# Retention attention, a gated layer and a two-layer MLP on one Trainium2 core: the rest scores of a pair moved behind the far parts, weight steps re-dealt, gelu's table loaded first

## The chip, the cores and the metric

The kernel runs on one core of one Trainium2 chip. The metric is device time in microseconds, the median of three runs; lower is better. The core has TensorE (PE, with its weight loads as PEld), VectorE (DVE), ScalarE (ACT), GpSimd (POOL), and SyncE (SP), whose queue issues every transfer of this kernel.

## What is computed

Three layers in a row, all in fp32 (products of the two later layers are made of three products of high and low halves):

```python
# attention: B, H, S, D = 4, 8, 576, 64
scores = q @ k.T / sqrt(64);  ret = scores * gamma_h ** (i - j)  (0 where i < j);  x = ret @ v
# gated layer: x is [4, 576, 512], d_ff = 1024
h = gelu_tanh(x @ w_in);  u, v = split(h);  v = layernorm(v) * g_ln
x = x + (u * (w_sg @ v + b_sg)) @ w_out
# two-layer MLP
x = x + relu((layernorm(x) * g_ln2) @ w_ch1) @ w_ch2
```

The weights w_in, w_out and w_ch reach the device as pairs of 32-bit words (float64) and are turned into fp32 there.

## The kernel before, in words

**Attention.** The 32 heads are taken as 16 units of two heads; `for k in range(NPAIR)` runs over eight pairs of units, a = 2k and b = 2k + 1. The 576 positions are four chunks of 128 and a rest of 64. For each unit `scores` makes the products of q and k within the chunks (L254; one PSUM bank for each head), `masks` multiplies them on DVE into p and frees these banks (L260), `states` makes k times v of each chunk (L294), `scans` runs the decayed sum over chunks on DVE (L304), `near` multiplies p with v (L316), and `far` adds the part that comes from earlier chunks (L325). The rest of 64 has its own steps, for both units of a pair in one bank: `scores_rest` (L273), `mask_rest` (L280) and `attend_rest` (L340). `finish(k)` is `far` and `put` (copy to SBUF by ACT, L347) of both units, then `attend_rest` and `put_rest` (L353). It runs one pair late: `finish(k - 1)` stands in the iteration of pair k. `scale_q` multiplies q by a row of decays on POOL, in two instructions: the four chunks (L241) and the rest (L243); this needs the scores to have been made, and `far` and `attend_rest` need it.

**PSUM.** There are eight banks. One is lent for good to the float64 conversion (`f64_at`), seven go round in a first-in, first-out list: `bank()` takes the oldest free one, `free` gives one back. While a pair runs, its four score banks, the two outputs of the pair ahead and the rest bank of the pair ahead are seven.

**Loads.** kk and qv tiles hold a unit's k and q with v; there are four kk and six qv buffers. The tiles of pair k + 2 are asked for in pair k, qv after `finish(k - 1)`, kk after `near`. All transfers are issued by SP in program order, so one that waits for its buffer holds up those behind it.

**Background.** `bg` is a generator that converts the weights in pieces of 512 columns, four steps a piece: a step that asks for the raw words two pieces ahead (L145) and makes the first DVE operation (L154); one that splits the piece before into high (ACT, L362) and low (POOL, L363) and makes the second DVE operation (L158); one with ACT's Square (L160) and DVE's third (L161); and one with DVE's last (L163). The very first step only asks for two raw pieces. Eight pieces are w_in, four w_out, and then w_ch follows to the end of the gated layer. `PAIR` says, for each pair, how many steps are made at its first place (ahead of `finish`) and at its last (behind `near`); `PACE` says the same for the gated layer.

**After attention.** `v_tile` makes the v half of the gated layer for batch 0: five products (tiles 0, 4, 1, 2, 3), each followed on ACT by gelu (L685), a squared sum (L670), the normalisation (L682) and the cast into a high half (L710); POOL makes the low half (L711). The steps of one tile's normalisation come some `tick`s after its gelu, between the next ones. `u_chunk` makes the u half (eight products of 12 matmuls), and `sg_chunk` multiplies w_sg with the normalised v: each half is 4 x 3 + 2 = 14 matmuls, the last of them with tile 4's low half (L788). `load_sg` and `split_sg` load and split the five row tiles of w_sg.

The lines of every instruction follow the order of the code; each engine works through its own in that order.

Of the kernel before, what the change touches and what calls it, by code (L numbers as in the profile page):

```python
# [14 lines left out]
ACTF = mybir.ActivationFunctionType  # L15
ALU = mybir.AluOpType
# [5 lines left out]
NP = H // 2  # L22
F1 = 1024
F2 = 2048
C = 128
NC = S // C
R = S - NC * C
# [17 lines left out]
    "1112",  # L45
)
LATE = 5
PAIR = "00 01 00 23 23 23 24 35".split()

HIDDEN = {  # L50
    5: (5, 0, True, True), 0: (0, 1, True, False), 1: (1, 1, False, True), 2: (2, 2, True, False),
# [23 lines left out]
O_LATE = H  # L75
# [26 lines left out]
def kernel(  # L102
# [28 lines left out]
    def col(t, o, n=1):  # L131
        return t[:, o:o + n]
# [104 lines left out]
    def scale_q(n):  # L237
        q = units[n]["qT"]
        row = col(tab, O_LATE + n % NP * C, C)
        x = q[:, 0:NC * C].rearrange("p (c i) -> p c i", c=NC)  # L240
        pool.tensor_tensor(out=x, in0=x, in1=row.unsqueeze(1).to_broadcast([128, NC, C]), op=ALU.mult)  # L241
        x = q[:, NC * C:]
        pool.tensor_tensor(out=x, in0=x, in1=row[:, 0:R], op=ALU.mult)  # L243

    half = [slice(h * D, (h + 1) * D) for h in range(2)]

    def scores(n):
        unit(n)
        u = units[n]
        u["sc"] = [bank() for h in range(2)]  # L250
        for c in range(NC):
            j = slice(c * C, (c + 1) * C)
            for h in range(2):
                pe.matmul(u["sc"][h][:, j], u["kT"][half[h], j], u["qT"][half[h], j], start=True, stop=True)  # L254

    def masks(n):
        u = units[n]
        p = u["p"] = pa.tile([128, 2, NC, C], F32, tag="p", name="p")
        for h in range(2):
            dve.tensor_tensor(  # L260
                out=p[:, h], in0=u["sc"][h].rearrange("p (c i) -> p c i", c=NC),
                in1=mask[:, 2 * (n % NP) + h].unsqueeze(1).to_broadcast([128, NC, C]), op=ALU.mult,
            )
            free(u["sc"][h])
# [3 lines left out]
    def scores_rest(k):  # L268
        t = rests[k] = bank()
        for x in range(2):  # L270
            u = units[2 * k + x]
            for r in half:
                pe.matmul(  # L273
                    t[r, x * R:(x + 1) * R], u["kT"][r, NC * C:], u["qT"][r, NC * C:], start=True, stop=True,
                    skip_group_check=True,
                )

    def mask_rest(k):
        pr = units[2 * k]["pr"] = pa.tile([128, 2 * R], F32, tag="pr", name="pr")
        dve.tensor_tensor(  # L280
            out=pr, in0=rests[k][:, 0:2 * R], in1=col(tab, O_MASKR + 2 * k % NP * R, 2 * R), op=ALU.mult
        )
# [47 lines left out]
    def attend_rest(k):  # L330
        for part in range(2):
            for x in range(2):
                u = units[2 * k + x]
                for r in half:
                    o = rests[k][r, (2 + x) * R:(3 + x) * R]
                    if part == 0:
                        w, z = u["v"][r, NC * C:], units[2 * k]["pr"][r, x * R:(x + 1) * R]
                    else:
                        w, z = u["y"][r, NC - 1], u["qT"][r, NC * C:]
                    pe.matmul(o, w, z, start=part == x == 0, stop=part == 1, skip_group_check=True)  # L340
# [9 lines left out]
    def put_rest(k):  # L350
        b, hp = divmod(2 * k, NP)
        t = rests.pop(k)
        act.copy(xb[b][:, hp:hp + 2, NC * C:], t[:, 2 * R:4 * R].rearrange("p (x i) -> p x i", x=2))  # L353
        free(t)
        for x in range(2):
            del units[2 * k + x]
# [26 lines left out]
    def load_sg(part):  # L383
        if part == 0:
            w = S + NC * C + D
            t = [ld.tile([128, w], F32, tag="qv", bufs=6, name="raw_sg") for _ in range(2)]
            sg.extend(x[:, i * S:(i + 1) * S] for x in t for i in range(2))
        else:
            sg.append(ld.tile([128, S + NC * C], F32, tag="kk", bufs=4, name="raw_sg")[:, 0:S])
        for k in range(part * NC, NC + part):  # L390
            nc.sync.dma_start(out=sg[k], in_=w_sg[k])

    def split_sg(k):
        if k == 0:
            for t in [slot("w_sg") for _ in range(3)]:
                sg_rows.extend(t[:, a * S:(a + 1) * S] for a in range(3))
        if k < NC:
            wsl.append((sg_rows[2 * k], sg_rows[2 * k + 1]))
            split(sg_rows[2 * k], sg_rows[2 * k + 1], sg[k])
        else:  # L400

            t = sg_rows[8]
            wsl.append(t)
            act.copy(t, sg[k])
            pool.tensor_tensor(out=t[R:, :], in0=sg[k][R:, :], in1=f(t[R:, :]), op=ALU.subtract)
# [79 lines left out]
    def background(n):  # L485
        for _ in range(n):
            next(bg, None)
# [22 lines left out]
    for n in range(1, 4):  # L510
        load(load_kk(n), load_qv(n))

    act.copy(zero[:, 0:1], zero[:, 0:1])

    warm = bank()
    for _ in range(WARM):
# [40 lines left out]
            out=to, in0=to, in1=first[:, O_GR:O_GR + NP].unsqueeze(2).to_broadcast([128, NP, R]), op=ALU.mult  # L557
        )

    def finish(k):  # L560
        for n in (2 * k, 2 * k + 1):
            far(n)
            put(n)
        attend_rest(k)
        put_rest(k)

    for k in range(NPAIR):
        a, b = 2 * k, 2 * k + 1
        if k == 0:
            form_rows()  # L570
            form_masks(0)
        scores(a)
        if k == 0:
            scale_k(a)
        masks(a)
        if k == 0:
            form_decay()
            form_late()
            free(each[0])
            states(a)  # L580
            near(a)
            form_masks(1)
            free(each[1])
        else:
            scale_k(a)
        if k == 1:
            finish(k - 1)
        scores(b)
        masks(b)
        scale_k(b)  # L590
        scores_rest(k)
        if k:
            mask_rest(k)
        scale_q(a)
        scale_q(b)
        background(int(PAIR[k][0]))
        if k > 1:
            finish(k - 1)
        if 0 < k < NPAIR - 2:
            load(load_qv(a + 4), load_qv(b + 4))  # L600
        if k == NPAIR - 2:
            load_sg(0)
        if k == NPAIR - 1:
            split_sg(0)
            split_sg(1)
        if k:
            states(a)
        states(b)
        scans(k)
        if k == 0:  # L610
            form_rest()
            mask_rest(k)
        if k:
            near(a)
        near(b)
        if k == 0:
            load(load_kk(4), load_qv(4), load_kk(5), load_qv(5))
        else:
            load(load_kk(a + 4), load_kk(b + 4))
        if k == NPAIR - 2:  # L620
            load_sg(1)
        background(int(PAIR[k][1]))
        if k == NPAIR - 3:
            nc.sync.dma_start(out=par, in_=params)
        if 1 < k < 6:
            split_x(0, [k - 2])
        if k == 6:
            split_rest(0)
    finish(NPAIR - 1)
    background(4)  # L630
    for k in range(2, NC + 1):
        split_sg(k)
    background(4)
    es_a.close()

# [927 lines left out]
```

## Time and profile before

| what | value |
|---|---|
| median of three runs | 661.36 us (660.23 to 662.06) |
| the profiled execution, device time | 659.58 us |
| its span | 657.7 us |
| PE busy in the span | 646.3 us (98%) |
| DVE / ACT / POOL busy | 456.3 / 316.8 / 321.7 us |
| granted TensorE clock | 1.0 in every slice (the 2.4 GHz level) |

The span is what the profile shows of the program; 1.88 us of the profiled execution lie around it. PE is busy nearly all the time, so what counts are the few places where it is not. The timeline of an engine gives start and length of each merged group of instructions, and in brackets the idle time before it with what ended it.

### The profile page before, as it was taken

To read this page: it belongs to the slowest core of one execution; us is meant where nothing else is said; L and a number is where in the kernel's file an instruction comes from. 1 tells how busy PE (TensorE), PEld (TensorE's weight loads), DVE (VectorE), ACT (ScalarE), POOL (GpSimd) and SP (SyncE) were. 2 spreads that over 40 slices of the span, in tenths; PEclk is the share of its full clock that TensorE was granted. 3 is DMA by queue.
4 is the path that set the end of the run, shared out by engine and by line. 5 is a ranking of instruction groups with operands and counts; after the bars stand their busy time and mean duration, and the time that the engine had idled before them with its cause. 6 is when DMAs were issued, how large, how long until landed. Compare 5 with 4: busy or idle time off the path is not lost.

```text
span 657.7 us, 12552 instructions
## 1 busy us (share of the span) xinstructions
PE 646.3 (98%) x4422; PEld 590.2 (90%) x4422; DVE 456.3 (69%) x907; ACT 316.8 (48%) x657; POOL 321.7 (49%) x314
## 2 busy tenths in 40 slices
PE   8999998999999999999999999999999999999997
PEld 5998898899889889899888899988998889999996
DVE  5599879789889885868888633555533445458894
ACT  4465795375276457434453533233535313335443
POOL 2567767235226527955655693365558842410000
PEclk9999999999999999999999999999999999999999
DMA  8999537677697695489896768699999799999734
GB/s 312 409 386 327 189 98 231 225 251 235 214 307 228 190 236 141 170 296 389 311 301 251 265 204 272 242 371 379 340 323 346 242 303 322 360 370 412 281 129 160
DMA packets 99264, 181.22 MB, mean 276 GB/s; under 512 B 9857, under 2 KB 46849, under 8 KB 97410
## 3 DMA queue, kind: packets, MB, share of 16 engines
q1 hardware_dynamic: 99202, 180.42, 80.6%
q8 instruction: 35, 0.57, 0.3%
q14 instruction: 27, 0.22, 0.1%
HBM read 122.97 MB, written 56.62 MB: 273 GB/s over the span
## 4 chain that ended last, share of the span: by engine, by line
PE 84%; DVE 6%; ACT 5%; issue 3%; POOL 2%; DMA 1%; DVEq 0%; SPq 0%; POOLq 0%; ACTq 0%
PE b L137 22%; PE b L136 22%; PE b L135 22%; PE b L854 6%; PE b L1331 3%; PE b L1332 2%; PE b L325 1%; PE b L254 1%; DVE b L154 1%; DVE c L163 1%; PE b L294 1%; ACT raw L160 1%; PE b L316 1%; POOL vnl L711 1%; PE b L788 1%
## 5 line engine op out<-in xcount | busy, mean ns | idle before, releaser
L135 PE MATMUL b<-fe,w 128*128 128x384 f32 x336 | 113.2, 337 | 0.0
L137 PE MATMUL b<-fe,w 128*128 128x384 f32 x336 | 113.0, 336 | 0.0
L136 PE MATMUL b<-fe,w 128*128 128x384 f32 x336 | 112.7, 335 | 0.0
L137 PE MATMUL b<-w,h 128*128 128x512 f32 (+1 forms) x270 | 98.1, 363 | 0.0
L136 PE MATMUL b<-w,h 128*128 128x512 f32 (+1 forms) x270 | 97.9, 363 | 0.0
L135 PE MATMUL b<-w,h 128*128 128x512 f32 (+1 forms) x270 | 96.8, 358 | 0.0
L935 POOL TENSOR_TENSOR w<-raw_w,w 128x512 fp32r<-128x512 f32 x30 | 39.9, 1332 | 57.9 <-ACT w L934 50.8
L135 PEld LDWEIGHTS b<-fe,w 128*128 128x128 f32 x336 | 63.1, 188 | 4.0 <-DVE t L1188 0.8
L136 PEld LDWEIGHTS b<-fe,w 128*128 128x128 f32 x336 | 63.1, 188 | 2.6
L137 PEld LDWEIGHTS b<-fe,w 128*128 128x128 f32 x336 | 63.0, 188 | 0.0
L137 PEld LDWEIGHTS b<-w,h 128*128 128x128 f32 x270 | 50.9, 189 | 7.7
L160 ACT ACTIVATE raw<-raw 128x512 f32<-128x512 f32 x44 | 29.9, 680 | 57.7 <-DVE b L158 47.6
L136 PEld LDWEIGHTS b<-w,h 128*128 128x128 f32 x270 | 50.9, 189 | 6.1
L135 PEld LDWEIGHTS b<-w,h 128*128 128x128 f32 x270 | 51.0, 189 | 6.0 <-issue 0.2
L1165 ACT ACTIVATE h<-b 128x384 fp32r<-128x384 f32 x32 | 15.7, 491 | 79.5 <-DVE b L1194 53.1
L655 POOL TENSOR_TENSOR st<-st,par 128x1 f32<-128x1 f32 x36 | 22.1, 616 | 50.4 <-DVE st L654 50.3
L951 POOL TENSOR_TENSOR raw_turn<-raw_turn 128x256 f32<-128x256 f32 x32 | 23.6, 739 | 31.1 <-DMA raw_turn<-w_dram 20.8
L137 PE MATMUL b<-w_sg,vnl 128*128 128x288 f32 x128 | 37.8, 295 | 0.5 <-POOL vnl L711 0.5
L1166 DVE SCALAR_TENSOR_TENSOR h<-b,h 128x384 fp32r<-128x384 f32 x32 | 17.8, 556 | 29.4 <-ACT h L1165 29.4
L135 PE MATMUL b<-w_sg,vnh 128*128 128x288 f32 x128 | 37.8, 295 | 0.0
L137 PE MATMUL b<-xt_hi,w_in 128*128 128x288 f32 x128 | 37.7, 295 | 0.0
L136 PE MATMUL b<-w_sg,vnh 128*128 128x288 f32 x128 | 37.7, 295 | 0.0
(200 smaller groups left out, 1716.4 us busy)
## 6 DMA issues: line engine op xcount, KB each, us to landing
w<-ws_dram SPq DMA_DIRECT2D x96, 256.0 KB, 5.1
raw<-in_w_ch_dram SPq DMA_DIRECT2D x32, 512.0 KB, 5.0
ws_dram<-w SPq DMA_DIRECT2D x16, 896.0 KB, 7.3
w<-wb_dram SPq DMA_DIRECT2D x14, 1024.0 KB, 6.2
qv<-in_attn_dram SPq DMA_DIRECT2D x15, 576.0 KB, 6.4
w_dram<-c SPq DMA_DIRECT2D x32, 256.0 KB, 3.1
wb_dram<-fe SPq DMA_DIRECT2D x32, 256.0 KB, 5.4
kk<-in_attn_dram SPq DMA_DIRECT2D x15, 544.0 KB, 7.3
```

What stands on the lines that cost most here:

```text
L135: pe.matmul(ps, lh, rh, start=first, stop=False, skip_group_check=True)
L136: pe.matmul(ps, lh, rl, start=False, stop=False, skip_group_check=True)
L137: pe.matmul(ps, ll, rh, start=False, stop=last, skip_group_check=True)
L160: act.activation(out=f(w1), in_=f(w1), func=ACTF.Square)
L655: pool.tensor_tensor(out=st[:, 4:5], in0=st[:, 3:4], in1=col(par, O_MH), op=ALU.pow)
L854: pe.matmul(ps, g, wo[k][:, w], start=done[0] == 1, stop=done[0] == 3 * KE, skip_group_check=True)
L935: pool.tensor_tensor(out=t[:, 1], in0=raw, in1=f(t[:, 0]), op=ALU.subtract)
L951: pool.tensor_tensor(out=to, in0=y, in1=z, op=ALU.subtract)
L1165: act.activation(out=t[:, 0], in_=v, func=ACTF.Relu)
L1166: dve.scalar_tensor_tensor(out=t[:, 1], in0=v, scalar=0.0, in1=f(t[:, 0]), op0=ALU.max, op1=ALU.subtract)
L1331: pe.matmul(ps, e[:, 0, x], t, start=begin, stop=False, skip_group_check=True)
L1332: pe.matmul(ps[:, 0:256], e[:, 1, x], t[:, 0:256], start=False, stop=end, skip_group_check=True)
```

## The change

`scores_rest(k)` moves into `finish(k - 1)`, between `attend_rest` and `put_rest`, for pairs 2 to 7 (pairs 0 and 1 keep it behind `scores(b)`). Since `scale_q` may not overwrite the rest of q before that, the rest's multiplication becomes `scale_rest`, and it and `mask_rest(k)` now follow `finish(k - 1)`. `PAIR` is re-dealt: the first step, which asks for the first two raw pieces of w_in, is made at the end of pair 0 and not of pair 1, every pair from the second on makes half a piece at its end and the other half in the next pair, and four steps that stood between the attention and the gated layer are dropped there, so they are made later. Four of the five splits of w_sg now stand in the last pair (before: two). The first ACT instruction, a copy of one zero, becomes a gelu of it.

```diff
-PAIR = "00 01 00 23 23 23 24 35".split()
+PAIR = "01 02 22 22 22 22 22 34".split()
...
-        x = q[:, NC * C:]
-        pool.tensor_tensor(out=x, in0=x, in1=row[:, 0:R], op=ALU.mult)
+
+    def scale_rest(n):
+        x = units[n]["qT"][:, NC * C:]
+        pool.tensor_tensor(out=x, in0=x, in1=col(tab, O_LATE + n % NP * C, R), op=ALU.mult)
...
-    act.copy(zero[:, 0:1], zero[:, 0:1])
+    act.activation(out=zero[:, 0:1], in_=zero[:, 0:1], func=ACTF.Gelu_apprx_tanh)
...
-    def finish(k):
+    def finish(k, more=True):
         for n in (2 * k, 2 * k + 1):
             far(n)
             put(n)
         attend_rest(k)
+        if more:
+            scores_rest(k + 1)
         put_rest(k)
...
         if k == 1:
-            finish(k - 1)
+            finish(k - 1, False)
         scores(b)
+        if k == 1:
+            scores_rest(k)
         masks(b)
         scale_k(b)
-        scores_rest(k)
-        if k:
-            mask_rest(k)
+        if k == 0:
+            scores_rest(k)
         scale_q(a)
         scale_q(b)
         background(int(PAIR[k][0]))
         if k > 1:
             finish(k - 1)
+        if k:
+            mask_rest(k)
+        scale_rest(a)
+        scale_rest(b)
...
         if k == NPAIR - 1:
-            split_sg(0)
-            split_sg(1)
+            for x in range(2):
+                split_sg(x)
...
+        if k == NPAIR - 1:
+            for x in range(2, NC):
+                split_sg(x)
         background(int(PAIR[k][1]))
...
-    finish(NPAIR - 1)
-    background(4)
-    for k in range(2, NC + 1):
-        split_sg(k)
+    finish(NPAIR - 1, False)
+    split_sg(NC)
     background(4)
```

How the instructions stand, at three places. First PE in the last pair, from its last score product on; b_80, b_82 and so on are PSUM banks. Before:

```order
L254 MATMUL b_77<-qv,kk 128x128
L273 MATMUL b_82<-qv,kk 64x64 x4
L325 MATMUL b_81<-qv,y 64x128 x6
L325 MATMUL b_79<-qv,y 64x128 x6
L340 MATMUL b_80<-pr,qv 64x64 x4
L340 MATMUL b_80<-qv,y 64x64 x4
L294 MATMUL b_76<-qv,kk 64x64 x16
```

and now:

```order
L256 MATMUL b_77<-qv,kk 128x128
L327 MATMUL b_81<-qv,y 64x128 x6
L327 MATMUL b_79<-qv,y 64x128 x6
L342 MATMUL b_80<-pr,qv 64x64 x4
L342 MATMUL b_80<-qv,y 64x64 x4
L275 MATMUL b_82<-qv,kk 64x64 x4
L296 MATMUL b_76<-qv,kk 64x64 x16
```

The rest scores into b_82 moved from ahead of the far parts to behind `attend_rest`; pairs 2 to 6 read alike. DVE beside it, from the scans of pair 6 to those of pair 7 (b_75 is the conversion's bank, p the masked scores). Before:

```order
L304 SCALAR_TENSOR_TENSOR y<-formed,b_77 128x256 x2
L158 SCALAR_TENSOR_TENSOR b_75<-raw,b_75 128x512
L161 SCALAR_TENSOR_TENSOR b_75<-raw,b_75 128x512
L163 SCALAR_TENSOR_TENSOR c<-raw,b_75 128x512
L154 TENSOR_SCALAR b_75<-raw 128x512
L260 TENSOR_TENSOR p<-b_82,formed 128x512
L260 TENSOR_TENSOR p<-b_76,formed 128x512
L260 TENSOR_TENSOR p<-b_78,formed 128x512
L260 TENSOR_TENSOR p<-b_77,formed 128x512
L280 TENSOR_TENSOR pr<-b_82,tab 128x128
```

and now:

```order
L306 SCALAR_TENSOR_TENSOR y<-formed,b_77 128x256 x2
L154 TENSOR_SCALAR b_75<-raw 128x512
L158 SCALAR_TENSOR_TENSOR b_75<-raw,b_75 128x512
L262 TENSOR_TENSOR p<-b_82,formed 128x512
L262 TENSOR_TENSOR p<-b_76,formed 128x512
L262 TENSOR_TENSOR p<-b_78,formed 128x512
L262 TENSOR_TENSOR p<-b_77,formed 128x512
L161 SCALAR_TENSOR_TENSOR b_75<-raw,b_75 128x512
L163 SCALAR_TENSOR_TENSOR c<-raw,b_75 128x512
L154 TENSOR_SCALAR b_75<-raw 128x512
L282 TENSOR_TENSOR pr<-b_82,tab 128x128
```

Two conversion operations instead of four now stand between the scans and the next masks, and two stand between the masks and the rest's mask (a third, L154, in the last pair only).

Second, ACT from the end of the last pair's copies to the first gelu of the gated layer (b_78, b_77 and b_82 hold the last pair's outputs). Before:

```order
L347 COPY xb<-b_78 128x512
L347 COPY xb<-b_77 128x512
L353 COPY xb<-b_82 128x2x64
L362 CAST w_in<-c 128x512
L160 ACTIVATE raw<-raw 128x512
L362 CAST w_in<-c 128x512
L362 CAST w_sg<-raw_sg 128x576 x2
L404 CAST w_sg<-raw_sg 128x576
L160 ACTIVATE raw<-raw 128x512
L646 ACTIVATE par<-par 128x8
L685 ACT_TABLE_LOAD
L685 ACTIVATE t,st<-b_81 128x512
```

and now:

```order
L349 COPY xb<-b_78 128x512
L349 COPY xb<-b_77 128x512
L355 COPY xb<-b_82 128x2x64
L406 CAST w_sg<-raw_sg 128x576
L364 CAST w_in<-c 128x512
L160 ACTIVATE raw<-raw 128x512
L364 CAST w_in<-c 128x512
L656 ACTIVATE par<-par 128x8
L695 ACTIVATE t,st<-b_81 128x512
```

Two w_sg casts, one Square and the table load have left this stretch.

Third, SP in the first pairs, from the kk tile of unit 4 on. Before:

```order
L210 DMA kk<-in_attn_dram 128x1088
L217 DMA qv<-in_attn_dram 128x1152
L210 DMA kk<-in_attn_dram 128x1088
L217 DMA qv<-in_attn_dram 128x1152 x3
L210 DMA kk<-in_attn_dram 128x1088 x2
L145 DMA raw<-in_w_in_dram 128x1024 x2
L217 DMA qv<-in_attn_dram 128x1152 x2
L210 DMA kk<-in_attn_dram 128x1088 x2
L145 DMA raw<-in_w_in_dram 128x1024
```

and now:

```order
L210 DMA kk<-in_attn_dram 128x1088
L217 DMA qv<-in_attn_dram 128x1152
L210 DMA kk<-in_attn_dram 128x1088
L217 DMA qv<-in_attn_dram 128x1152
L145 DMA raw<-in_w_in_dram 128x1024 x2
L217 DMA qv<-in_attn_dram 128x1152 x2
L210 DMA kk<-in_attn_dram 128x1088 x2
L145 DMA raw<-in_w_in_dram 128x1024
L217 DMA qv<-in_attn_dram 128x1152 x2
```

The first two raw pieces now go ahead of the tiles of units 6 and 7, and from then on one raw piece more than before is ahead of each pair's tiles.

## Rows read from the trace of the kernel before

**Rows 1.** Busy us by engine in three stretches, then clock, DMA share, GB/s

```profile
core 0: us, PE busy (x) PEld busy (x) DVE busy (x) ACT busy (x) POOL busy (x), PEclk, DMA share, GB/s
...
22.52:71.44 48.92, 46.92 (x907) 44.38 (x905) 41.19 (x70) 28.02 (x59) 33.59 (x36) 1.00 0.94 351
...
97.86:102.62 4.76, 2.64 (x16) 1.98 (x15) 4.03 (x7) 3.74 (x9) 4.11 (x4) 1.00 0.79 215
102.62:600.00 497.38, 497.25 (x2736) 456.38 (x2736) 334.75 (x662) 225.36 (x460) 259.25 (x246) 1.00 0.84 280
```

**Rows 2.** PE's waits over the span: total us, times, longest us

```profile
PE b L273 <- DVE p L260: 2.0, 4, 1.1
PE b L788 <- POOL vnl L711: 1.5, 1, 1.5
```

**Rows 3.** PE timeline of pair 2: start, length, line, form; no wait inside

```profile
22.52 2.06 PE L254 MATMUL b<-qv,kk 64*128 64x128 f32 x32
...
24.80 1.65 PE L325 MATMUL b<-qv,y 64*64 64x128 f32 x24
...
27.08 1.15 PE L294 MATMUL b<-qv,kk 128*64 128x64 f32 x32
...
29.91 2.06 PE L254 MATMUL b<-qv,kk 64*128 64x128 f32 x32
```

**Rows 4.** PE timeline: starts of pairs 4, 5 and 7, and the last far parts

```profile
37.30 2.06 PE L254 MATMUL b<-qv,kk 64*128 64x128 f32 x32
...
45.09 2.06 PE L254 MATMUL b<-qv,kk 64*128 64x128 f32 x32
...
60.55 2.06 PE L254 MATMUL b<-qv,kk 64*128 64x128 f32 x32
...
69.10 1.71 PE L325 MATMUL b<-qv,y 64*64 64x128 f32 x24
```

**Rows 5.** DVE timeline: scans, masks of pair 3, a conversion step, masks of pair 7

```profile
28.27 1.26 DVE L304 TENSOR_TENSOR_SCAN y<-formed,b 128x256 f32<-128x256 f32 x2 [1.83 <-PE b L294]
...
31.16 2.48 DVE L260 TENSOR_TENSOR p<-b,formed 128x512 f32<-128x512 f32 x4 [1.62 <-issue]
...
62.37 0.69 DVE L154 TENSOR_SCALAR b<-raw 128x512 uint32<-128x512 uint32 x1
62.97 2.47 DVE L260 TENSOR_TENSOR p<-b,formed 128x512 f32<-128x512 f32 x4
```

**Rows 6.** PE timeline: first product of the u half, first of w_sg

```profile
85.14 0.29 PE L135 MATMUL b<-xt_hi,w_in 128*128 128x288 f32 x1
...
97.86 0.29 PE L135 MATMUL b<-w_sg,vnh 128*128 128x288 f32 x1
```

**Rows 7.** ACT timeline around the end of attention, first and fifth gelu

```profile
68.02 1.29 ACT L362 CAST w_sg<-raw_sg 128x576 fp32r<-128x576 f32 x2
...
75.47 1.25 ACT L362 CAST w_sg<-raw_sg 128x576 fp32r<-128x576 f32 x2
...
77.97 1.28 ACT L685 ACT_TABLE_LOAD   x1
79.26 0.60 ACT L685 ACTIVATE t<-b 128x512 f32<-128x512 f32 x1
...
88.04 0.59 ACT L685 ACTIVATE t<-b 128x512 f32<-128x512 f32 x1
```

**Rows 8.** POOL timeline: the last low half of v in batch 0

```profile
101.08 1.26 POOL L711 TENSOR_TENSOR vnl<-t,vnh 128x512 fp32r<-128x512 f32 x1
```

**Rows 9.** DMA issues at 14.08 (unit 5) and 20.45 (unit 6): KB, us to landing

```profile
qv<-in_attn_dram SPq DMA_DIRECT2D x1, 576.0 KB, 8.3
...
kk<-in_attn_dram SPq DMA_DIRECT2D x1, 544.0 KB, 6.4
```

**Rows 10.** As rows 1, two stretches of attention: DMA at its fullest and thinnest

```profile
12.00:30.00 18.00, 17.83 (x338) 16.31 (x334) 11.80 (x22) 8.47 (x19) 9.42 (x12) 1.00 1.02 410
...
50.00:53.00 3.00, 3.00 (x68) 2.83 (x68) 2.49 (x4) 0.89 (x3) 2.98 (x4) 1.00 0.82 266
```

**Rows 11.** SP's own waits in the first 130 us

```profile
SPq L217 <- PE b L340: 20.1, 5, 4.7
```

## The prediction, made before the changed kernel was run

> **What bounds the kernel now.** I read the busy time by stretches first. From 102.62 us to 600 us PE is busy for 497.25 of 497.38 us at the 2.4 GHz level [rows 1]: nothing that another engine does there can bring time, as long as it stays hidden. Time is lost in two places ahead of that. PE's waits name them [rows 2]: the rest scores (L273) wait four times for DVE's masks, and the last product of the first w_sg half (L788) waits for POOL's low half of v.
>
> A wait understates its loss, so I take the loss from starts. A pair without a wait takes 29.91 - 22.52 = 7.39 us [rows 3]. Pair 4 took 7.79 us, pairs 5 and 6 together 15.46 us, and the last one, up to its own far parts, 8.55 us [rows 4]: 0.40 + 0.68 + 1.16 = 2.24 us lost. In the gated layer the u half makes 96 products in 97.86 - 85.14 = 12.72 us, 0.1325 us each [rows 6]; the first w_sg half, 14 products, should take 1.86 us and took 4.76 us [rows 1]: 2.90 us lost. So 5.1 us is the most that the change can give.
>
> **The rest scores.** Seven banks are all in use when the last score product is issued, so the rest scores need the bank that the first mask frees. DVE begins the masks 1.25 us after the start of pair 3, but 2.42 us after that of pair 7 (31.16 and 62.97) [rows 3 to 5]: there up to four conversion operations of 0.72 us (0.69 [rows 5] and the step between them) stand between the scans and the masks. The change puts the far parts and the rest's sums, 27.08 - 24.80 = 2.28 us [rows 3], ahead of the rest scores, and these need no bank. The bank is then asked for over 4 us after the pair's start; the first mask (2.48 / 4 = 0.62 us) is done 3.04 us after it in the worst pair of before. Even that lateness is covered by 1 us, and with two conversion operations ahead of the masks instead of four it shrinks.
>
> What is late next? DVE has 1.26 us of scans, 2.48 us of masks [rows 5], four conversion operations (2.9 us) and the rest's mask (less than one mask, 0.62) in each pair: at most 7.2 of 7.39 us, so it keeps up, with little to spare. The second unit's scores need the bank that the scans free. States end about 4.56 + 1.15 us into the pair [rows 3], scans 1.3 us later, at 7.0 us; the bank is asked for 1 us into the next pair, at 8.4 us: 1.4 us of cover. mask_rest behind two conversion operations still ends before states do, and is needed a pair later. On POOL the rest's multiplication goes behind `finish`, also a pair ahead of its use. All this costs nothing while these covers hold.
>
> **The raw w_in ahead of units 6 and 7.** In SP's order two raw tiles of 512 KB now go ahead of the qv and kk tiles of units 6 and 7. The tile ahead of them landed at 14.08 + 8.3 = 22.4 us [rows 9], and the DMA was full, at 410 GB/s [rows 10], so each raw tile takes 1.28 us. Unit 6's kk, landed at 20.45 + 6.4 = 26.85 us [rows 9], comes at 29.4 us and is needed at 29.91; unit 7's comes 1.36 us later, at 30.8, and is needed at 30.9. That is a cover of 0.5 and 0.1 us; if I am out by a transfer, PE waits up to 0.6 us. From then on one raw tile more is ahead of each pair. A pair's tiles and one raw tile are 2752 KB, 6.9 us at 410 GB/s, under 7.39 us, so the lateness doesn't grow. The first raw tile lands at 23.7 us, and DVE's two operations on it now stand ahead of pair 2's masks, which begin at 25.2 instead of about 23.8 us; the scans then end near 30.5 us, 0.4 us before their bank is wanted. I take 0.1 us for all this: of the 2.24 us, 2.1 us come back; the ends are 2.24 and 1.5.
>
> **The first w_sg half.** The low half that PE waits for ends at 101.08 + 1.26 = 102.34 us [rows 8], 14.30 us after the fifth gelu began at 88.04 [rows 7]. That gelu's product was done when the u half began, about 85.3 us: ACT was 2.7 us late. The order of ACT and POOL between this gelu and that low half is the same in both kernels, so the 14.30 us stay. PE asks for the low half 13 products into w_sg, at 97.86 + 1.72 = 99.58 us. Had the fifth gelu begun with its product, the low half would end at 99.6. So all of the 2.90 us but 0.1 to 0.2 go if ACT gains 2.7 us on PE; each microsecond that is missing comes back as a wait.
>
> Attention ends near 69.10 + 2.28 = 71.4 us and the first gelu began at 79.26 [rows 4, 7], 7.9 us later. What stood between: the last two w_in pieces, three w_sg casts, the table load. Now two w_sg casts (1.25) and the load (1.28) [rows 7] are gone from there, and the conversion is half a piece further on: behind the scans, which end some 2.5 us before attention does, DVE has seven operations left, 5.1 us with their handovers from ACT. That is 2.6 us past attention's end, then a cast about as long as a gelu (0.60 us [rows 7]) and a small scaling, in all 3.5 to 4 us. A v product takes (85.14 - 71.4) / 5 = 2.75 us [rows 6], so the first is there 3 us after attention, and ACT starts about 1 us late instead of 5: a gain of about 4 us where 2.7 are needed. From first to fifth gelu ACT took 8.8 us [rows 7], now with one piece fewer to cast; 4 + 8.8 is less than the 13.9 us (five products and the handover) after which the fifth is done. I take 2.7 us back; the ends are 2.9 and 0, set by ACT.
>
> The load itself isn't saved, it changes place: the first one of the kernel stood at the start anyway. The row has 1.28 us, and the gelu begins right behind it, so 1.28 us is what leaves ACT's queue here. The Trainium skill ("ScalarE: Activation LUTs", What ACT_TABLE_LOAD costs) counts 1.28 us and a drain of 1.38 us for each switch of tables, 2.66 us in all. The trace shows no drain of that size between its neighbours, so the row decides; by the page ACT's margin would be 1.4 us wider and the first rival below a little less likely, with the same sum.
>
> **Later.** Four steps, one piece, are made later than before: four DVE operations (2.9 us), a Square and a cast. They go into the stretch where DVE is busy for 334.75 and ACT for 225.36 of 497 us [rows 1]. I cost them at nothing; uncovered they are 2.9 us.
>
> **The sum.** 2.1 + 2.7 = 4.8 us, less 0.1 for a chain that I may have missed: 4.7 us. The profiled execution took 659.58 us, so 654.9 us; the median of the runs is 1.78 us above it, and from that I get 661.36 - 4.7 = **656.7 us**.
>
> **Rivals.**
> ACT stays late. All four w_sg casts now stand ahead of two w_in casts in ACT's queue; before, the first two ran at 68.02 [rows 7]. If the w_sg tiles land no earlier than that, ACT waits some 3.3 us there, the fifth gelu is 1.6 us late, and 1.7 of the 2.9 us stay. For it: SP asks for those tiles only behind an attend_rest, and its queue waits there up to 4.7 us [rows 11]. Against: that attend_rest now comes earlier in its pair. 2.1 + 1.2 = 3.3 us: 658.1 us.
>
> The wait only moves. DVE has 0.2 us a pair to spare by my bound; if its handovers from ACT take more, the scans' or the second mask's bank is late in place of the first, and the change doesn't do what it says there. Only the w_sg part is left: 658.7 us. Against: the lateness of before grew over four operations in a row, which are now two and two.
>
> Nothing measurable: both of these together, or the later piece uncovered, 660 to 661.4 us.
>
> Slower: the transfers become the bound. The DMA moved 410 GB/s early but 266 GB/s at 50 to 53 us [rows 10]. If the second is what it can do beside the other engines, a pair's 2.82 MB take longer than PE's 7.39 us. With four pairs to go and about 1.4 us in hand, the loss passes the 4.7 us of gain once a pair takes 1.5 us more, 8.9 us: under 317 GB/s. At 300 GB/s a pair takes 9.4 us, 4 x 2.0 - 1.4 = 6.6 us lost: 663.3 us. For it: one raw tile more is always ahead. Against: that stretch was thin because SP's next qv waits for PE [rows 11], and with a full queue the rate was 410.
>
> **How the numbers follow.** Forecast 0.56 (656.7, by itself 655.2 to 658.0), ACT late 0.17, wait moved 0.10, nothing measurable 0.10, slower 0.07. A measurement of this kernel tells about 0.3% (2.0 us) from no change: below 659.4 is faster. That holds for the forecast, most of the first rival and most of the second: 0.78; same 0.16, slower 0.06. For 8 in 10 the range takes in the first two rivals and leaves out the last two: 655.0 to 659.8 us.
>
> **What would show it.** No wait of L275 (the old L273) among PE's waits, and pairs 3 to 7 of 7.4 us each; a first gelu some 4 us behind attention's end and no second table load; less than 0.5 us of wait at the first w_sg half. I am wrong if PE waits for kk or qv in pair 3 or later, for a bank of the scans, or if the fifth gelu starts over 1 us behind its product.

## The result: slower by half a per cent, where faster was forecast

The changed kernel takes 664.38 us (median of four runs, 663.94 to 665.89) against 660.89 us beside it: a ratio of 1.0055, 95% interval 1.0032 to 1.0078. The forecast was 656.7 us, the range 655.0 to 659.8, and slower had 6 chances in 100. The profiled execution took 663.94 us, its span 662.0 us (before: 657.7).

Both gains that the prediction counted on are there in the trace. So are two losses, one of which it had priced at nothing.

First the busy times of the stretches, as in [rows 1] (columns as there, after the stretch and its length: PE, its weight loads, DVE, ACT, POOL, the granted clock, DMA share, GB/s), of the kernel after:

```profile
22.50:71.60 49.10, 47.69 (x919) 45.08 (x915) 42.34 (x72) 31.38 (x63) 35.68 (x38) 1.00 0.94 355
...
97.60:102.62 5.02, 4.98 (x38) 4.74 (x37) 4.82 (x9) 4.11 (x9) 5.02 (x5) 1.00 0.87 220
102.62:248.00 145.38, 145.25 (x873) 132.76 (x873) 123.70 (x266) 75.17 (x171) 56.78 (x62) 1.00 0.77 237
248.00:264.00 16.00, 12.27 (x75) 11.23 (x74) 8.11 (x20) 11.39 (x22) 10.25 (x8) 0.89 0.35 93
264.00:600.00 336.00, 335.92 (x1739) 307.31 (x1738) 197.65 (x369) 135.23 (x260) 189.94 (x176) 1.00 0.89 303
```

The first w_sg half (97.60 to 102.62) has lost its gap: PE is busy for 4.98 of 5.02 us, where it had 2.64 of 4.76. A new gap stands at 248 to 264 us, in the last batch's first w_sg halves: 3.7 us of PE are idle and the clock's mean is 0.89. The kernel before has no idle time there:

```profile
248.00:264.00 16.00, 16.00 (x123) 16.00 (x122) 9.09 (x13) 11.13 (x23) 13.08 (x8) 1.00 0.54 147
```

PE's waits (total us, times, longest) say on what, and answer to [rows 2]:

```profile
PE b L135 <- ACT vnh L720: 1.9, 1, 1.9
PE b L137 <- POOL vnl L721: 1.8, 3, 0.8
PE b L256 <- DMA kk<-in_attn_dram: 1.4, 2, 1.2
PE b L526 <- DMA grow<-in_row_dram: 0.4, 1, 0.4
```

No rest scores (L275 now) and no last low half (L798 now) are left among them. Here are the starts of pairs 2, 3, 4, 5 and 7 and of the last far parts on PE's timeline, as in [rows 3, 4]:

```profile
23.20 2.06 PE L256 MATMUL b<-qv,kk 64*128 64x128 f32 x32
...
31.89 1.16 PE L256 MATMUL b<-qv,kk 64*128 64x128 f32 x16 [1.25 <-DMA kk<-in_attn_dram]
33.23 1.16 PE L256 MATMUL b<-qv,kk 64*128 64x128 f32 x16 [0.17 <-DMA kk<-in_attn_dram]
...
39.72 2.06 PE L256 MATMUL b<-qv,kk 64*128 64x128 f32 x32
...
47.10 2.06 PE L256 MATMUL b<-qv,kk 64*128 64x128 f32 x32
...
61.88 2.06 PE L256 MATMUL b<-qv,kk 64*128 64x128 f32 x32
...
69.27 1.71 PE L327 MATMUL b<-qv,y 64*64 64x128 f32 x24
```

From pair 4 on every pair takes 7.38 or 7.39 us, the length of an undisturbed pair. Pair 2 took 8.69 us, since pair 3's first scores waited 1.25 us for kk, and pair 3 took 7.83. Pair 2 itself began 0.68 us later than before; 0.43 of it is the wait for grow, a load near the start of the kernel. Two kernels below that are identical up to the end of attention (y2 and y3) differ by 0.49 us there, so I count it as variation between executions.

ACT's timeline shows the first and the fifth gelu, as in [rows 7]:

```profile
74.82 0.62 ACT L364 CAST w_in<-c 128x512 fp32r<-128x512 f32 x1 [1.17 <-DVE c L163]
75.35 0.20 ACT L656 ACTIVATE par<-par 128x8 f32<-128x8 f32 x1
75.46 0.58 ACT L695 ACTIVATE t<-b 128x512 f32<-128x512 f32 x1
...
85.51 0.60 ACT L695 ACTIVATE t<-b 128x512 f32<-128x512 f32 x1 [0.58 <-PE b L137]
```

The first gelu begins 3.86 us behind the end of attention (71.60) instead of 7.8, with no table load ahead of it. The fifth waits for PE, not PE for it.

**The account.** Start against start on PE, after minus before: +0.68 us at pair 2, +0.16 at the end of attention, -2.45 at the end of the first w_sg half's products, -2.43 when batch 3's w_sg products begin (252.25 us), +3.96 at 262 us, +4.3 at the end. So: 0.68 of the start, 1.30 + 0.44 in pairs 2 and 3, -2.26 by the rest scores, -2.61 by the first w_sg half, 0.35 in small pieces, and **6.4 us in batch 3's first w_sg halves** (the expectations of the experiments, written before, have 6.2).

**Where the 6.4 us come from.** Four engines' timelines of the kernel after, in the order of the chain: SP's issues, DVE, ACT, PE.

```profile
236.85 4.82 SPq L1007 DMA_DIRECT2D x_raw<-z_dram  x8
241.77 8.16 SPq L438 DMA_DIRECT2D w_dram<-c  x3
```

```profile
243.02 0.69 DVE L161 SCALAR_TENSOR_TENSOR b<-raw,b 128x512 uint32<-128x512 uint32 x1
248.89 0.69 DVE L163 SCALAR_TENSOR_TENSOR c<-raw,b 128x512 f32<-128x512 f32 x1 [5.18 <-DMA w_dram<-c]
249.50 0.15 DVE L664 TENSOR_SCALAR st<-st 128x1 f32<-128x1 f32 x1
```

```profile
250.36 0.81 ACT L692 ACTIVATE t<-t,st 128x512 f32<-128x512 f32 x1 [5.13 <-DVE st L689]
```

```profile
255.56 0.40 PE L135 MATMUL b<-w_sg,vnh 128*128 128x288 f32 x1 [1.91 <-ACT vnh L720]
...
256.91 0.40 PE L137 MATMUL b<-w_sg,vnl 128*128 128x288 f32 x1 [0.81 <-POOL vnl L721]
...
258.58 0.61 PE L137 MATMUL b<-w_sg,vnl 128*128 128x288 f32 x1 [0.83 <-POOL vnl L721]
258.98 0.45 PE L797 MATMUL b<-w_sg,vnh 128*128 128x288 f32 x1
259.22 0.45 PE L798 MATMUL b<-w_sg,vnl 128*128 128x288 f32 x1
```

The four late steps have moved a piece of w_ch into batch 3's v tiles: three conversions stand there instead of two. The staging tile c has two buffers, so the third conversion's last operation (L163) needs the first one's store (L438) to be done. That store was issued at 241.77, behind the eight loads of the MLP's features (L1007), and landed at 248.8. DVE stood still for 5.18 us, with the steps of the tiles' normalisation queued behind; ACT got their numbers 5.13 us late, and PE reached w_sg before the normalised v. PE is idle for 3.7 us in these waits. From start to start, with the products right behind each wait, they cost 4.9 us up to 258.58 us. The other 1.5 us are the clock: from there to 261.6 us the products follow each other by 0.24 us, where a product of this form takes 0.1325 us [rows 6].

### The profile page after: what moved, and what is told of

Same layout as the page of the kernel before. It is cut to its first block, busy times and chain, and to the rows that moved or that the text cites. A ratio compares the mean times of both kernels' runs of the same rounds, so it can differ in the third digit from the quotient of the medians.

```text
span 662.0 us, 12555 instructions
## 1 busy us (share of the span) xinstructions
PE 649.0 (98%) x4422; PEld 591.7 (89%) x4422; DVE 454.7 (69%) x907; ACT 317.0 (48%) x656; POOL 321.2 (49%) x314
## 4 chain that ended last, share of the span: by engine, by line
PE 69%; DVE 11%; DMA 10%; ACT 4%; issue 3%; POOL 2%; SPq 1%; DVEq 0%; ACTq 0%; POOLq 0%
PE b L137 17%; PE b L135 17%; PE b L136 17%; PE b L864 4%; PE b L1341 3%; PE b L256 2%; DMA x_r<-x_dram 2%; DMA kk<-in_attn_dram 2%; PE b L327 2%; PE b L318 2%; PE b L1342 2%; DMA ws_dram<-w 1%; DVE c L163 1%; DMA raw_w<-w_dram 1%; DMA x<-z_dram 1%
## 5 line engine op out<-in xcount | busy, mean ns | idle before, releaser
L160 ACT ACTIVATE raw<-raw 128x512 f32<-128x512 f32 x44 | 29.9, 679 | 50.1 <-DVE b L158 45.4
L721 POOL TENSOR_TENSOR vnl<-t,vnh 128x512 fp32r<-128x512 f32 x18 | 23.3, 1298 | 29.9 <-ACT vnh L720 25.0
```

What stands on the lines that cost most here:

```text
L160: act.activation(out=f(w1), in_=f(w1), func=ACTF.Square)
L721: pool.tensor_tensor(out=vl[:, i], in0=t, in1=f(vh[:, i]), op=ALU.subtract)
```

## The experiments

Twelve kernels, each with the kernel before run on the same chip. The kernels y, z and w answer what the first four (x) left open.

| kernel | median us | before us | ratio (95%) |
|---|---|---|---|
| x1_steps_before_batch3 | 662.82 | 661.67 | 1.0023 (1.0007 to 1.0038) |
| x2_one_raw_early | 663.19 | 661.67 | 1.0027 (1.0010 to 1.0044) |
| x3_both | 661.69 | 661.67 | 1.0008 (0.9990 to 1.0026) |
| x4_before_less_four | 664.80 | 661.67 | 1.0050 (1.0032 to 1.0068) |
| y1_four_after_attention | 657.43 | 660.38 | 0.9942 (0.9921 to 0.9963) |
| y2_four_and_one_raw | 656.77 | 660.38 | 0.9934 (0.9912 to 0.9956) |
| y3_four_in_w_out_0 | 657.86 | 660.38 | 0.9967 (0.9952 to 0.9983) |
| y4_half_features_later | 658.83 | 660.38 | 0.9971 (0.9952 to 0.9991) |
| z1_rest_scores_alone | 661.43 | 661.25 | 0.9997 (0.9977 to 1.0016) |
| z2_w_sg_and_table_alone | 659.50 | 661.25 | 0.9977 (0.9962 to 0.9993) |
| z3_no_raw_in_first_pairs | 658.87 | 661.25 | 0.9959 (0.9943 to 0.9975) |
| w1_late_steps_both_queues | 658.00 | 660.67 | 0.9952 (0.9933 to 0.9971) |

**x4: the kernel before, with the four steps alone left for later.**

```diff
     finish(NPAIR - 1)
-    background(4)
     for k in range(2, NC + 1):
```

> The kernel before, with one background(4) behind the attention taken away and nothing else. Theory A: a third conversion stands beside batch 3's v tiles and DVE waits 5 us for a c buffer there; PE loses about 6 us near 256 us, and gains up to 1.2 us of the 2.9 us at the first w_sg half, since ACT has a piece less: about 660.9 + 5 = 666 us. Rival B: no wait in batch 3, 660 us.

It is slower by as much as the changed kernel, and the same instruction waits for the same store (DVE's timeline; then the stretch 246 to 262 us, columns as above):

```profile
250.44 0.69 DVE L163 SCALAR_TENSOR_TENSOR c<-raw,b 128x512 f32<-128x512 f32 x1 [5.31 <-DMA w_dram<-c]
```

```profile
246.00:262.00 16.00, 12.79 (x79) 11.62 (x78) 5.29 (x16) 10.63 (x24) 6.78 (x7) 0.84 0.61 146
```

On PE it gains 2.4 us at the first w_sg half, twice what was expected, and loses 6.7 us in batch 3 (by PE's starts against the kernel before). Nothing else of the change is in this kernel, so the late steps alone are enough for the result.

**y4: what holds the staging buffer.** The changed kernel; half of the features' loads are asked for one v tile later.

```diff
-            for h in range(2):
-                load_features(0, h)
+            load_features(0, 0)
...
             v_tile(b, i)
+            if last and i == 1:
+                load_features(0, 1)
```

> The changed kernel, with the four loads of the second half of the features (x_raw from z_dram) asked for one v tile later, behind the first store of a converted piece, so that this store has four of the strided loads ahead of it in the queue instead of eight. No arithmetic moves. If batch 3's wait comes from that store holding the staging buffer c (A's chain), it lands about 4 us sooner, DVE's wait of 5.2 us falls to about 1, PE's waits in batch 3's first w_sg halves go nearly, and the time is 659.5. If the extra piece's own DVE and ACT work is the cause, whatever the queue, the waits stay and the time is 664.

```profile
235.85 2.09 SPq L1007 DMA_DIRECT2D x_raw<-z_dram  x4
238.04 0.41 SPq L438 DMA_DIRECT2D w_dram<-c  x1
238.49 2.79 SPq L1007 DMA_DIRECT2D x_raw<-z_dram  x4
```

```profile
243.78 0.69 DVE L163 SCALAR_TENSOR_TENSOR c<-raw,b 128x512 f32<-128x512 f32 x1 [1.06 <-DMA w_dram<-c]
```

The store is issued 3.7 us sooner than in the changed kernel and lands 5.1 us sooner, at 243.65 us. DVE's wait falls from 5.18 to 1.06 us and the time by 5.5 us (from 1.0055 to 0.9971 of before), with the same arithmetic in the same order. So the place of the store in the queue, not the work of the extra piece, cost 5.5 of the 6.4 us. A wait of 0.6 us for the low half of v stays there.

**x1 and x3: the four steps made one stage sooner, at the end of batch 1's w_out** (x3 also with x2's edit).

```diff
-    ("27122", "2433", "2142", "13530"),
+    ("27122", "2433", "2142", "13534"),
```

> The changed kernel with four more background steps at the end of batch 1's w_out (0 becomes 4 there), so that batch 3's v tiles have two conversions beside them, as before the change, and not three. Theory A (the deferred piece: its last DVE operation waits for a c buffer whose store stands behind the feature loads, and holds up the normalisation): the 5.2 us wait of DVE and the 6.2 us that PE loses near 253 to 261 us go; 664.2 - 6.2 = 658 us. Rival B (the early part now runs some 2.5 us ahead and meets the feature loads at a worse moment, whatever the number of pieces): the wait stays, about 664 us.

> Both edits on the changed kernel. If both theories hold, the gains of the change are left: 2.2 us in attention and 2.6 us at the first w_sg half, 660.9 - 4.8 = 656.1 us. If only the batch 3 theory holds, 657.7; if only the kk theory holds, 662.6.

Batch 3 is whole again, and the loss stands in batch 2's first w_sg halves: 5.6 us in x1, 5.9 in x3, by PE's starts. The stretch 196 to 214 us of x1, and the DVE row ahead of it from which the lateness starts:

```profile
196.00:214.00 18.00, 14.84 (x93) 13.76 (x92) 16.49 (x45) 13.58 (x26) 9.99 (x11) 0.91 0.70 211
```

```profile
194.12 0.69 DVE L163 SCALAR_TENSOR_TENSOR c<-raw,b 128x512 f32<-128x512 f32 x1 [1.21 <-ACT raw L160]
```

The four operations now sit in a row right ahead of batch 2's normalisation. The last waits 1.21 us for a Square (L160) that ACT makes behind the v tile's own squares, and DVE comes 4 us late to the steps of the normalisation (the first, L685, at 195.38 us; in the changed kernel at 191.01). This is read from the two traces; no run tries it by itself. So x1's expectation failed: moving the steps ahead of batch 3 was not enough, they must also not stand in a v tile's rush.

**x2: one raw tile of w_in instead of two in the first pair**, and the second in a step of its own in the next (the third argument, new in `f64_pieces`, asks for that step).

```diff
-PAIR = "01 02 22 22 22 22 22 34".split()
+PAIR = "01 03 22 22 22 22 22 34".split()
...
-        yield from f64_pieces(load_w_in())
+        yield from f64_pieces(load_w_in(), 1, 1)
```

> The changed kernel with one raw w_in tile, not two, ahead of the tiles of units 6 and 7; the second is asked for behind them (one background step more in pair 1). Theory A (pair 3 waits because the raw tiles stand ahead of unit 6's kk in one full queue): the 1.25 us and 0.17 us waits for kk go, 664.2 - 1.6 = 662.6 us, and the wait of batch 3 stays. Rival (unit 6's kk came late because its transfer was issued 0.7 us later in that execution): a wait of some 1 us stays, 664 us.

No wait for kk is left in pair 3; batch 3's wait is there as in the changed kernel. The ratio falls from 1.0055 to 1.0027, 1.9 us, for a wait of 1.4 us: the intervals are too wide to tell these apart. One early tile is not free either: pairs 2 to 4 still take 1.1 us more than undisturbed ones (8.10, 7.53 and 7.68 us; y2, which begins in the same way, has 8.09, 7.54 and 7.59), and in pair 2 PE now waits 0.2 us each for DVE's masks ahead of the rest scores and the states. In z3 below, with no early tile, pairs 2 to 4 take 7.38 or 7.39 us. In the kernels with two raw tiles the wait was 1.4 us (after), 1.5 (x1), 0.8 (y1) and 0.2 us (y4): its size changes from execution to execution.

**y1 to y3: the four steps back where there is room.** In y1 `background(4)` behind the last `split_sg` becomes `background(8)`; y2 has x2's edit too; y3 has x2's edit and puts the four steps into batch 0's w_out:

```diff
-    ("14203", "1414", "2430", "32323"),
+    ("14203", "1414", "2430", "52523"),
```

> The changed kernel with the four steps of the weights' conversions put back at the end of attention: eight steps behind the last part of w_sg, where the changed kernel has four. Everything behind the first batch's v tiles then stands as in the kernel before. Theory A (the four steps that came late cost the 6 us of batch 3): no wait of PE in batch 3's nor in batch 2's first w_sg halves, and the four steps hide under the first v tiles, where DVE is idle 2.7 us between 76 and 80 us; 664.4 less 6.2 is 658.2, and the wait of pair 3 for kk (1.4 us) is still there. Rival (the four steps hid nothing at the end of attention either, so that the gain of the first w_sg half was bought with them): batch 3's wait is gone, but 2 us or more of the first w_sg half's wait at 98 us are back, 660.5.

> The same, and one raw tile of w_in instead of two asked for in the first pair, as in x2_one_raw_early. Theory A with the late kk in pair 3 as the second loss: 658.2 less 1.4, 656.8 us, with no wait of PE over 0.3 us in pairs 2 to 4, in the first w_sg halves of batches 0, 2 and 3. The rival of the run before, if it holds: 659 us, with the wait at 98 us back.

> The kernel of x2_one_raw_early (663.2 us) with the four late steps in batch 0's w_out instead: two more behind its first tile and two more behind its third. Theory A asks only that they are done before batch 3's v tiles and don't stand in the v tiles' own rush: DVE is 2.0 of 4 us busy at 116 to 120 us, so they are hidden there, no wait appears in batches 1 to 3, and the time is 657 us. Rival (DVE has no such room anywhere between 100 and 250 us, and any four steps more make the next w_sg half wait, as x1 and x3 showed for batch 2): a wait of 4 us or more stands in batch 1's, 2's or 3's first w_sg halves, 661 us.

All three came within 0.9 us of what theory A said; y3 has a wait of 0.3 us in batch 1's first w_sg half, where none was expected. **y2 beats both kernels**: 656.77 us, 0.9934. These are the waits of PE that its trace lists between 10 and 280 us, and the stretch of batch 3:

```profile
PE b L318 <- DVE p L262: 0.5, 3, 0.2
PE b L296 <- DVE p L262: 0.2, 1, 0.2
PE b L275 <- DVE p L262: 0.2, 1, 0.2
```

```profile
248.00:264.00 16.00, 16.00 (x123) 16.00 (x122) 10.96 (x16) 9.27 (x19) 15.21 (x11) 1.00 0.54 157
```

The changed kernel had no need to make these steps later: the gain of the first w_sg half is the same 2.6 us by PE's starts with them (y1 and y2; y3 has them elsewhere).

**w1: the steps left late, both queues mended** (x2's and y4's edits).

> The changed kernel with its four late steps left late, and both queues mended: one raw tile instead of two in the first pair (x2_one_raw_early), and half of the features' loads one v tile later (y4_half_features_later). If these two queues are all that the prediction missed, both predicted gains stand and the ratio to the kernel before is that of the prediction, 656.7 to 661.4, 0.993; and four steps made late cost nothing of themselves. If late steps cost in other places too (DVE and ACT short of room in batch 3), it stays at y4's 0.997 or above, with PE's waits in batch 3 of 1 us or more.

The ratio, 0.9952, lies between y2's and y4's, and its interval holds both. By PE's starts it is 4.26 us ahead of the kernel before at 102 us, and then gives back 1.2 us in batch 3's first w_sg halves and 0.8 in the w_out behind, with waits of 0.8 us for v's low half and 0.5 us in w_out. So its expectation failed both ways: the late steps are not free even then, but they cost less than the other branch said. Half of the features' loads moved aside is not all of their price. Between w1 and y2 the intervals don't decide.

**z1: the rest scores alone** (the kernel before with `scale_rest`, `finish(k, more)` and the order of the masks from the diff, the rest as it was).

> The kernel before with the move of the rest scores alone (their scaling, masks and products as in the changed kernel); raw tiles, w_sg, gelu's table and the conversions' steps stand as before. Theory (this part did what the prediction said): the wait of PE for y ahead of the rest scores in pairs 3 to 7 is gone, each of these pairs takes 7.4 us instead of 7.7, no kk is late, 660.4 less 1.5 to 2.2 is 658.6. Rival (the gain in attention is taken back at the first w_sg half at 98 us, where ACT sets the time in the kernel before): no change, 660.4, with that wait 2 us longer.

The rival's time came, but not in the way that it named. In attention PE gains 1.66 us from pair 2's start to the end, and the median doesn't move; yet the wait at 98 us is not 2 us longer. z1's and then before's stretch from 98 to 108 us, and z1's waits there:

```profile
98.00:108.00 10.00, 7.51 (x40) 6.75 (x39) 8.93 (x17) 6.46 (x15) 8.36 (x8) 0.83 0.78 226
```

```profile
98.00:108.00 10.00, 7.88 (x56) 7.22 (x55) 9.04 (x17) 6.50 (x15) 8.37 (x8) 1.00 0.84 239
```

```profile
PE b L797 <- POOL vnl L720: 1.5, 1, 1.5
PE b L137 <- POOL vnl L720: 0.8, 1, 0.8
```

Only 0.4 us came back as a longer wait (0.55 from start to start), but the clock's mean fell to 0.83 and the products behind the waits ran 0.24 us apart from 103.2 to 106.4 us: 1.5 us more. All ten executions of z1 show this lower mean clock (0.997 or less over the whole execution). Of the 25 of the kernel before beside it 14 do, and these take 662.2 us in the mean, 0.8 more than z1's 661.4. So part of the gain is still there when like is set against like.

**z2: w_sg, the table and the steps behind them alone** (the kernel before with `split_sg` of 2 to 4 in the last pair, the last one and `background(8)` behind attention, gelu first). **z3: y1 with the order of steps in attention of the kernel before** (`PAIR` as it was, so no raw tile in the first pair).

> The kernel before with w_sg split in the last pair, gelu's table loaded first, and the eight steps behind the last part of w_sg; attention's order and raw tiles as before. Theory: the wait of the first w_sg half at 98 us is gone, 2.7 of its 2.9 us back, and attention unchanged: 657.7. Rival (w_sg's copies on ACT between the last pair's own make the last pair later): 659.

> y1_four_after_attention (657.4 us) with the steps in attention where the kernel before has them, so that no raw tile is asked for ahead of kk of units 6 and 7. Both gains (the rest scores and the first w_sg half) with neither loss: no wait for kk in pair 3, none in batch 3; 660.4 less 2.1 less 2.7 is 655.6, no more than y2_four_and_one_raw's 656.8. Rival (the early raw tile bought something: the steps made in pairs 1 to 7 are fewer early and crowd the last pairs): a new wait in pairs 4 to 7, 658.

Both are faster than before and both fall short, mainly for one reason: the wait for the last low half is still there, 1.5 us in z2 and this in z3.

```profile
PE b L798 <- POOL vnl L721: 1.6, 1, 1.6
```

The first gelu of z2 begins at 78.79 us, only 0.47 earlier than before [rows 7], and that of z3 at 78.54, against 76.36 in y2. What holds it there is DVE's conversion of the last w_in pieces, not ACT's queue: ACT is idle for 1.9 and 0.9 us ahead of that gelu in both, waiting for DVE (and DVE 1.2 us for POOL's split of the piece before). With the first raw tiles asked for in the first pairs the conversion is further on. z3 also gains less in attention, 1.3 us, with a wait of 0.4 us for a scan in the last pair. z3's expectation that the early raw tile buys nothing was wrong: at the first w_sg half z3 gains 0.8 us by PE's starts and y1, the same kernel with the early tiles, 2.6; one of the two tiles is enough (y2).

## Point by point: the prediction against the runs

**Held: the rest scores.** No wait of L275, pairs 4 to 7 of 7.39 us; 2.26 us came back where 2.24 were lost (2.05 in y2, 1.66 in z1, and 1.3 in z3, which is below the lower end of 1.5). The four terms of DVE's bound add up to 7.26 us, not 7.2, so the margin was 0.13 us a pair. The covers named for scans, masks and POOL held in the changed kernel all the same; in z1 and z3 PE waits 0.2 and 0.4 us for a scan in the last pair.

**Held: the first w_sg half.** 2.7 us were taken, 2.61 came. The first gelu was forecast 4 us behind attention and came 3.86. The sharing out is new: w_sg and the table alone give 1.2 us of it (z2), the four dropped steps alone 2.4 (x4), and the change with its re-dealt `PAIR` but no step dropped all 2.6 (y1, y2). The prediction had put the gain down to ACT's queue and the half piece in one sum, and did not see that how far the conversion is weighs more than the queue.

**Failed: "Four steps, one piece, are made later ... I cost them at nothing; uncovered they are 2.9 us".** This step decided the sign. It cost 6.4 us, over twice its own upper bound. Two things were wrong with it. It read the room from the mean of a 497 us stretch [rows 1], though the piece lands in one place, batch 3's v tiles, which the order of the two programs shows. And it priced the piece by the length of its operations, 2.9 us, where the price is that of the resource it asks for: a staging buffer whose store stands behind eight other transfers. Neither bound of the term held the second kind of price, so it wasn't in the range either.

**Failed: "I take 0.1 us for all this" (the raw tiles).** It cost 1.3 + 0.4 us in the changed kernel's profile. The step that broke is the landing of unit 6's kk: 29.4 us forecast, 31.76 measured. Of these 2.4 us, 0.8 came with the tile ahead of the raw ones, which landed that much later than in the kernel before, and 1.7 between the two raw tiles, which landed 2.94 us apart where the forecast had 1.28. The DMA moved 359 GB/s at 22 to 26 us where the forecast had 410 [rows 10]; that alone is some 0.5 us (an estimate: 4 us at the one rate instead of the other). "If I am out by a transfer, PE waits up to 0.6 us" was also mis-added: with covers of 0.5 and 0.1 us, a transfer of 1.28 us leaves 0.8 us of wait for unit 6 and 1.2 in all; it was out by nearly two transfers, and PE waited 1.4 us. The issue rows (KB, median us to landing) of unit 6's kk, issued at 21.12, and of the two raw tiles in the kernel after, against [rows 9]:

```profile
kk<-in_attn_dram SPq DMA_DIRECT2D x1, 544.0 KB, 10.6
...
raw<-in_w_in_dram SPq DMA_DIRECT2D x2, 512.0 KB, 10.2
```

Why the rate dips there, and why the second raw tile lands so late, is not settled.

**The rivals.** "The transfers become the bound" gave 663.3 us and the sign that came, but by another mechanism: the lateness of kk didn't grow past pair 3, and attention as a whole ended only 0.16 us later than before. "The later piece uncovered" was named within "nothing measurable", with 2.9 us. With both losses mended, at 656.77 us against 660.38 (y2), the gain is 3.6 us in the medians and 3.0 between the profiled spans, of the 4.7 forecast. The medians say more because the kernel before runs part of its executions with a lower clock (last section); its executions beside y2 with a mean clock of 0.999 or more take 659.8 us in the mean, 3.0 above y2. By PE's starts y2 has nearly all of both gains, 2.05 + 2.60, less 0.71 at the start and 0.85 in short waits of pairs 2 and 3.

## What to carry to other kernels

Work that is moved later has to be looked up where it lands, in the order of instructions there, and priced by what it needs at that place: its buffers, what they wait for, and what is queued behind it on its engine, not by the mean load of the stretch. A store that frees a staging buffer is only as fast as the queue ahead of it. A gain ahead of a fixed wait can vanish in that wait and in the clock behind it (z1), so gains must be tried together with what follows them.

## What the runs showed of the hardware that was not expected

**The clock behind short waits.** In the changed kernel's batch 3 four stretches of 4 us read as follows:

```profile
248.00:252.00 4.00, 4.00 (x33) 4.00 (x32) 2.93 (x12) 1.61 (x3) 1.19 (x3) 1.00 0.29 103
252.00:256.00 4.00, 1.91 (x12) 1.32 (x10) 1.65 (x4) 3.97 (x9) 1.61 (x2) 1.00 0.49 120
256.00:260.00 4.00, 2.36 (x10) 1.91 (x10) 0.71 (x1) 3.97 (x10) 3.61 (x3) 0.79 0.54 134
260.00:264.00 4.00, 4.00 (x26) 4.00 (x26) 2.82 (x4) 1.84 (x4) 3.84 (x3) 0.78 0.06 15
```

PE waited 2.1 us and then 1.6 us; the products from 258.6 to 261.6 us ran 0.24 us apart, at the level of 1.2 GHz, and then again at 2.4 GHz. Idle times of 3.7 us in all cost 6.4 us from start to start, 1.5 of them at the lower clock.

**The kernel before also shows the lower clock, in some executions.** Of its 104 executions beside these experiments 48 show a mean clock of 1.000 and take 660.0 us on average (659.0 to 661.8); 51 show 0.997 or less and take 662.4 (661.1 to 665.0). The profiled one has 1.000. The place is likely the first w_sg half, since the kernels without that wait or with less of it (y1 to y4, z2, w1; 58 executions) never fall below 0.998, and z1, with a little more of it, shows 0.997 or less in all ten. z3, with the one wait of 1.6 us, has 0.997 once in ten. No trace of the kernel before with the lower clock was taken, so the place is not shown.

**A full queue of 512-byte rows moved half of the rate.** From 241 to 247 us, with the features' loads under way and a DMA share of 1.23, the DMA line of the changed kernel reads

```profile
DMA packets 2353, 1.21 MB, mean 202 GB/s; under 512 B 96, under 2 KB 2316, under 8 KB 2353
```

against 410 GB/s in attention [rows 10], where the packets have 4 KB and more. These loads move rows of 128 float32, 512 bytes each. The Trainium skill ("DMA: Bandwidth & Descriptors", Specifications) gives 512 B as the least size for the full rate. Here packets of that size moved 202 GB/s with the queue full, so the measurement differs from the page, if it is their size that counts: the rows also lie apart in DRAM, and no run here tells size from stride. The store of the staging buffer, 256 KB behind these loads, landed 7.0 us after its issue.
